# Lower halves of w2 moved from GpSimd to VectorE, the flag sums one half step later, an item's last tile scaled and stored by ScalarE

## The chip, the cores and the metric

One core of a Trainium2 chip runs the whole program. The metric is the device time of one execution in microseconds (us), the median of several runs. Engines are named as in the profile: PE is TensorE, PEld its weight loads, DVE is VectorE, ACT is ScalarE, POOL is GpSimd, SP is the engine that issues most DMAs.

## The reference, cut to what matters

A random-feature attention (4 batches, 8 heads, 576 positions, head size 64, 128 features) gives x of 2304 rows by 512. A mixture of 8 experts follows, one expert for each row:

```python
logits = x @ w_gate
expert_idx = np.argmax(logits, axis=1)
gate_w = probs[np.arange(N), expert_idx]        # softmax of logits
disp[e, counts[e]] = x[i]                       # up to `capacity` rows an expert
h = np.maximum(np.einsum('ecd,edf->ecf', disp, w1), 0.0)
y = np.einsum('ecf,efd->ecd', h, w2)
out[i] = gate_w[i] * y[expert_idx[i], pos[i]]   # zero where not kept
```

## The kernel before, in words

The first half (to about 103 us) is the attention. Its rows x are written to DRAM (x_d). Then come the *items*: a block of 576 rows (one batch) that is run through one expert, j = 0 to 3. Item 0 (block 0, with the expert of its first row) is started before the routing is known; how many of the other blocks have rows for the expert of their first row, and which expert that is, is found on the device by `route()`. The program branches on that count (L802); in this profile items 0, 1 and 2 run and item 3 doesn't. Rows that no item covers would go through lists (L930 and on), a branch that isn't taken here.

An item has two parts. In the first, `mm1` (L607) makes h = relu(x w1) in 16 *half steps*: 8 columns f of 128, and for each two halves of 288 rows. Every product is made as three matmuls, upper times upper, lower times upper and upper times lower (L614 to L616), where the *upper part* of a tile is its rounded copy (ACT, L125) and the *lower part* the rest (a subtraction, L128). A half step is 12 matmuls; then ACT writes the upper part of h (L619, and L621 in second halves) and DVE the lower (L622). In the second part, `mm2_rest` (L754) and `mm2` (L742) multiply by w2, one tile of 128 rows (the rest: 64) after another. `finish` (L769) scales a tile by its gate weights and `put` (L807) stores it. Between these tiles the next item's rows, which `prefetch` (L810) has loaded to xg, are transposed by PE (L347) and split by ACT (L351) and DVE (L353), and its w1 is split.

The lower parts of w2 (four pieces of 128x1024) are placed by the table LO_AT: piece c of w2 is split after column f. For item 0 they run on POOL (L840), for the others on DVE.

Item 0's half steps are interleaved with `route()`: after each, `listing(5)` (L788) takes up to five of its steps, and a step that yields "pe" ends the batch, so that what follows stands behind the next half step. `route()` makes the counts and gate weights on DVE (L369 to L444), spreads the weights to `sc_b` on ACT (L453), makes flags (L456, L458), and PE sums these flags over the rows with one small matmul, called `fs` (L462, preceded by "pe" at L459). From the sums DVE makes the numbers in `resd` (L465 to L510): which expert and which block each further item has. SP loads them (L814, L815) and issues the loads of xg (L338) and of w1 and w2 (L315) for item 1. All engines run their instructions in the order in which the program issues them; there is no scheduler that reorders.

At an item's end `finish` scales tile 3 (i == NSUB - 2) half on ACT (L779) and half on DVE (L781), and SP stores it. The order in which tiles are finished is 4, 0, 1, 2, 3.

```python
                for i, c in LO_AT[j > 0].get(f, ()):
                    split_w_lo(i, c, nc.gpsimd if j == 0 else nc.vector)
```

Of the kernel before, what the change touches and what calls it, by code (L numbers as in the profile page):

```python
# [14 lines left out]
ALU = mybir.AluOpType  # L15
# [4 lines left out]
B, H, S, D, M = 4, 8, 576, 64, 128  # L20
N, DM, E, FF = B * S, H * D, 8, 1024
# [3 lines left out]
SLOTS = 576  # L25
FIRST_CUTS = [0, 128, 384, 768, 1152]
SUB = 128
NSUB = 5
# [11 lines left out]
WARM = 3  # L40

HI_AT = ({2: ((2, 0),), 3: ((2, 1),), 4: ((2, 2),), 5: ((2, 3),)}, {0: ((2, 0),), 1: ((2, 1),), 3: ((2, 2),), 4: ((2, 3),)})
LO_AT = ({2: ((2, 0),), 3: ((2, 1),), 4: ((2, 2),), 5: ((2, 3),)}, {1: ((2, 0),), 2: ((2, 1),), 5: ((2, 2),), 6: ((2, 3),)})


def pause(n):
# [5 lines left out]
def attention_moe(ctx, tc, kT, qT, va, om, wg, w1, w2, cap, ident, tri, desc, lst, tab0, out):  # L52
    nc = tc.nc
# [12 lines left out]
    def bank(i, name):  # L66
        return ps.tile([128, 512], F32, tag=f"b{i}", name=name, bufs=1)
# [36 lines left out]
    resd = const.tile([1, 3, 4], I32, name="resd")  # L104
# [22 lines left out]
    def split_lo(lo, raw, hi, eng=None):  # L127
        (eng or nc.vector).tensor_tensor(lo, raw, hi.bitcast(F32), op=ALU.subtract)  # L128
# [156 lines left out]
    def zero_out(k):  # L285
        if k == 0:
            nc.sync.dma_start(out[SLOTS : SLOTS + REST, :], zero_sb[0:REST, :])
            return
        t = NSUB + 3 * (k - 1)
        z = min(t + 3, NT)  # L290
        nc.sync.dma_start(
            out[t * 128 : z * 128, :].rearrange("(a p) d -> p a d", p=128),
            zero_sb.unsqueeze(1).to_broadcast([128, z - t, DM]),
        )
# [15 lines left out]
    def load_w(i, c, ev):  # L310
        if i == 1:
            src = w1[ds(ev, 1), :, c * 256 : (c + 1) * 256].rearrange("o (k p) f -> p (o k) f", p=128)
        else:
            src = w2[ds(ev, 1), c * 256 : (c + 1) * 256, :].rearrange("o (k p) f -> p (o k) f", p=128)
        nc.sync.dma_start(w_raw[i][c], src)  # L315

    def split_w_hi(i, c, eng=None):
        split_hi(w_hi[i][c], w_raw[i][c], eng)

    def split_w_lo(i, c, eng=nc.vector, k=None):  # L320
        sl = slice(None) if k is None else slice(k, k + 1)
        split_lo(w_lo[i][c][:, sl, :], w_raw[i][c][:, sl, :], w_hi[i][c][:, sl, :], eng)
# [14 lines left out]
    def load_x(row):  # L337
        nc.sync.dma_start(big["xg"], x_d[ds(row, SUB * NSUB), :].rearrange("(i p) d -> p i d", p=SUB))  # L338
# [21 lines left out]
    def route():  # L360
# [21 lines left out]
        src, step = oh, 1  # L382
        while step < T:
# [4 lines left out]
            src, step = dst, 2 * step  # L388
# [68 lines left out]
        yield  # L457
        nc.vector.tensor_scalar(fl[:, 0 : B * NSUB], sc_b.rearrange("p b i -> p (b i)"), 0.0, None, op0=ALU.is_gt)  # L458
        yield "pe"  # L459
        fs = bank(SM, "fs")  # L460
        nf = B * NSUB + T
        nc.tensor.matmul(fs[:, 0:nf], ones_b, fl, start=True, stop=True)  # L462
# [144 lines left out]
    def mm1(f, n, hhi, hlo, hf, nm):  # L607
        xhi, xlo = big["xhi"], big["xlo"]
        whi_, wlo_ = w_hi[1][f // 2], w_lo[1][f // 2]
        fs = slice((f % 2) * 128, (f % 2) * 128 + 128)  # L610
        sl = slice(n * HS, (n + 1) * HS)
        pt = bank((2 * f + n) % 3, f"h{nm}{f}{n}")[:, 0:HS]
        for k in range(4):
            nc.tensor.matmul(pt, whi_[:, k, fs], xhi[:, k, sl], start=(k == 0), stop=False)  # L614
            nc.tensor.matmul(pt, wlo_[:, k, fs], xhi[:, k, sl], start=False, stop=False)  # L615
            nc.tensor.matmul(pt, whi_[:, k, fs], xlo[:, k, sl], start=False, stop=(k == 3))  # L616
        w = HS if n == 0 else HS - REST
        sl = slice(n * HS, n * HS + w)
        nc.scalar.activation(hhi[:, f, sl], pt[:, 0:w], AF.Relu)  # L619
        if n == 1:  # L620
            nc.scalar.activation(hf[:, f, :], pt[:, w:HS], AF.Relu)  # L621
        nc.vector.scalar_tensor_tensor(  # L622
            hlo[:, f, sl], pt[:, 0:w], 0.0, hhi[:, f, sl].bitcast(F32), op0=ALU.max, op1=ALU.subtract
        )

    def h_tiles(nm):
        return [
            hpool.tile([128, 8, w], dt, tag=t, name=f"{t}{nm}")
            for t, w, dt in (("hhi", 4 * SUB, F32R), ("hlo", 4 * SUB, F32R), ("hf", REST, F32))
        ]  # L630
# [7 lines left out]
    for n in range(NK + NT + 3):  # L638
# [6 lines left out]
        elif t < NT:  # L645
            pj = [bank((2 * t + i) % 3, f"pjq{n}{i}") for i in range(2)]
            c = max(i for i in range(len(QB) - 1) if QB[i] <= t)
# [121 lines left out]
    def finish(i, pt, nm, scale, put):  # L769
        n = sub_n[i]  # L770
        y = hpool.tile([SUB, DM], F32, tag="y", name=f"ys{nm}{i}", bufs=3)
        src = pt
        if n < SUB:
            src = y
            nc.scalar.copy(y[0:n, :], pt[n : 2 * n, :])
            nc.vector.tensor_tensor(y[0:n, :], pt[0:n, :], y[0:n, :], op=ALU.add)

        c = DM // 2 if i == NSUB - 2 else DM
        nc.scalar.mul(y[0:n, 0:c], src[0:n, 0:c], scale[0:n])  # L779
        if c < DM:  # L780
            nc.vector.tensor_scalar(y[0:n, c:], src[0:n, c:], scale[0:n], None, op0=ALU.mult)  # L781
        put(i, n, y)


    il = chain(*(g for g, _ in tasks), route())
    stop = [None]

    def listing(n):  # L788
        stop[0] = None
        for _ in range(n):  # L790
            if stop[0] is None:
                stop[0] = next(il, 0)
                if stop[0] == 0:
                    return

    row, nd, nl = None, None, None
    with ExitStack() as ifs:
        for j in range(B):
            nm = f"i{j}"
            last = j == B - 1  # L800
            if j > 0:
                ifs.enter_context(tc.If(nd > j - 1))  # L802
            hhi, hlo, hf = h_tiles(nm) if j > 0 else h0
            out_j = out[0:SLOTS, :] if j == 0 else out[ds(row, SLOTS), :]
            sc = sc_b[:, 0, :] if j == 0 else sc_j[:, j - 1, :]

            def put(i, n, y, out_j=out_j):  # L807
                nc.sync.dma_start(out_j[i * SUB : i * SUB + n, :], y[0:n, :])

            def prefetch():  # L810
                nonlocal row
                if last:
                    return
                ev = nc.sync.value_load(resd[0:1, 0, j : j + 1], min_val=0, max_val=E - 1)  # L814
                row = nc.sync.value_load(resd[0:1, 1, j : j + 1], min_val=0, max_val=N - S)  # L815
                load_x(row)
                for c in range(4):
                    load_w(1, c, ev)
                yield
                for c in range(4):  # L820
                    load_w(2, c, ev)
                yield

            pre = prefetch()
            if j > 0:
                next(pre, 0)
            h = 0
            for f in range(8):
                for half in range(2):
                    if j > 0 or (f, half) not in AHEAD:  # L830
                        mm1(f, half, hhi, hlo, hf, nm)
                        h += 1
                        if j == 0:
                            listing(5)
                for i, c in HI_AT[j > 0].get(f, ()):
                    split_w_hi(i, c)
                if j == 0 and f < 6:
                    zero_out(f)
                for i, c in LO_AT[j > 0].get(f, ()):
                    split_w_lo(i, c, nc.gpsimd if j == 0 else nc.vector)  # L840
            if j == 0:
                for _ in il:
                    pass
                next(pre, 0)
            for n, i in enumerate((NSUB - 1, *range(NSUB - 1))):
                pt = mm2(i, hhi, hlo, nm) if n > 0 else mm2_rest(hf, nm)
                if n == 0:
                    next(pre, 0)
                    finish(i, pt, nm, sc[:, i : i + 1], put)
                if n < 4 and not last:  # L850
                    split_w_hi(1, n)
                if n > 0:
                    finish(i, pt, nm, sc[:, i : i + 1], put)
                if not last:
                    for _ in transpose_x(n, f"i{j + 1}", SM if n % 2 else None):
                        pass
                if n < 4 and not last:
                    split_w_lo(1, n)
            if j == 0:
                nd = nc.values_load(resd[0:1, 2, 0:1], min_val=0, max_val=B - 1)  # L860
                nl = nc.values_load(resd[0:1, 2, 1:2], min_val=0, max_val=N)
# [154 lines left out]
```

## Time and profile before

| | us |
|---|---|
| median of 3 runs (283.48, 284.91, 285.92) | 284.91 |
| the profiled execution, its own time | 284.08 |
| its span, first to last instruction | 282.2 |

A row of a timeline gives the start and the busy time in us, engine, line, operation, output and inputs, the shape, and in brackets the idle time of the engine just before it and what ended that. A row of waits gives the total, the times and the longest. The granted clock of PE is given as a share of its full 2.4 GHz, so 0.50 is 1.2 GHz. Starts and ends of matmuls are modelled and overlap: in a steady stream the distance of two starts is what counts.

### The profile page before, as it was taken

To read this page: it belongs to the slowest core of one execution; us is meant where nothing else is said; L and a number is where in the kernel's file an instruction comes from. 1 tells how busy PE (TensorE), PEld (TensorE's weight loads), DVE (VectorE), ACT (ScalarE), POOL (GpSimd) and SP (SyncE) were. 2 spreads that over 40 slices of the span, in tenths; PEclk is the share of its full clock that TensorE was granted. 3 is DMA by queue.
4 is the path that set the end of the run, shared out by engine and by line. 5 is a ranking of instruction groups with operands and counts; after the bars stand their busy time and mean duration, and the time that the engine had idled before them with its cause. 6 is when DMAs were issued, how large, how long until landed. Compare 5 with 4: busy or idle time off the path is not lost.

```text
span 282.2 us, 7654 instructions
## 1 busy us (share of the span) xinstructions
PE 267.4 (95%) x3106; PEld 234.4 (83%) x3106; DVE 155.5 (55%) x326; ACT 150.0 (53%) x374; POOL 46.2 (16%) x58
## 2 busy tenths in 40 slices
PE   7899999999999999988999999999999999999980
PEld 5688898889899898978868889996888999958860
DVE  1998888678899875774523234443442262514230
ACT  1788778898899874344353415342731345343320
POOL 2100000233379890063300000000000000000000
PEclk9999999999999999997999999999999999999997
DMA  6999760046876844690598015901720293045111
GB/s 187 373 363 302 268 220 5 2 151 179 273 241 225 288 172 130 222 353 4 170 360 312 37 63 183 313 2 58 259 77 37 52 364 107 0 150 202 42 42 51
DMA packets 28450, 48.26 MB, mean 171 GB/s; under 512 B 2098, under 2 KB 14770, under 8 KB 28402
## 3 DMA queue, kind: packets, MB, share of 16 engines
q1 hardware_dynamic: 28258, 47.58, 50.1%
q8 instruction: 28, 0.46, 0.7%
q14 instruction: 20, 0.16, 0.2%
q10 hardware_dynamic: 144, 0.07, 0.1%
HBM read 35.71 MB, written 11.93 MB: 169 GB/s over the span
## 4 chain that ended last, share of the span: by engine, by line
PE 86%; DMA 5%; DVE 2%; issue 2%; ACT 1%; SPq 1%; DVEq 0%; ACTq 0%
PE hi L614 9%; PE hi L615 9%; PE hi L616 9%; PE kacc L212 7%; PE yi L747 7%; PE yi L749 7%; PE yi L748 7%; PE qacc L577 6%; PE pjq L158 6%; PE pjk L158 6%; PE qtr L658 3%; PE xtri L347 3%; DMA kraw<-kT 2%; DMA qraw<-qT 2%; PE yi2r L759 1%
## 5 line engine op out<-in xcount | busy, mean ns | idle before, releaser
L614 PE MATMUL hi<-xhi,w1hi 128*128 128x288 f32 x192 | 58.2, 303 | 0.0
L615 PE MATMUL hi<-xhi,w1lo 128*128 128x288 f32 x192 | 57.3, 299 | 0.0
L616 PE MATMUL hi<-xlo,w1hi 128*128 128x288 f32 x192 | 57.1, 297 | 0.0
L619 ACT ACTIVATE hhii<-hi 128x288 fp32r<-128x288 f32 (+1 forms) x48 | 18.4, 384 | 46.6 <-PE hi L616 46.6
L622 DVE SCALAR_TENSOR_TENSOR hloi<-hi,hhii 128x288 fp32r<-128x288 f32 (+1 forms) x48 | 20.3, 423 | 40.1 <-ACT hfi L621 24.3
L747 PE MATMUL yi<-w2hi,hhii 128*128 128x512 f32 x96 | 38.5, 401 | 0.0
L749 PE MATMUL yi<-w2lo,hhii 128*128 128x512 f32 x96 | 37.5, 391 | 0.0
L748 PE MATMUL yi<-w2hi,hloi 128*128 128x512 f32 x96 | 37.3, 389 | 0.0
L614 PEld LDWEIGHTS hi<-xhi,w1hi 128*128 128x128 f32 x192 | 36.7, 191 | 0.4
L615 PEld LDWEIGHTS hi<-xhi,w1lo 128*128 128x128 f32 x192 | 36.7, 191 | 0.0
L616 PEld LDWEIGHTS hi<-xlo,w1hi 128*128 128x128 f32 x192 | 36.7, 191 | 0.0
L353 DVE TENSOR_TENSOR xlo<-xtri,xhi 128x512 fp32r<-128x512 f32 (+1 forms) x20 | 12.7, 634 | 36.9 <-ACT xhi L351 36.9
L699 POOL TENSOR_TENSOR d<-d,mx 128x512 f32<-128x512 f32 x18 | 18.7, 1039 | 57.6 <-DVE mx L164 43.8
L164 DVE TENSOR_REDUCE mx<-pjk 128x4 f32<-128x512 f32 x36 | 23.1, 683 | 7.2 <-PE pjk L158 6.9
L685 ACT ACTIVATE ex<-pjk,mx 128x128 f32<-128x128 f32 x72 | 20.5, 368 | 8.0 <-DVE mx L164 7.8
L158 PE MATMUL pjk<-om_s,kraw 64*128 64x128 f32 x288 | 22.2, 291 | 2.1 <-DMA kraw<-kT 1.3
L577 PE MATMUL qacc<-kv_sb,qpT 128*64 128x73 f32 x576 | 22.5, 229 | 0.1
L212 PE MATMUL kacc<-v,ex 128*64 128x65 f32 (+1 forms) x576 | 22.3, 230 | 0.0
L158 PEld LDWEIGHTS pjk<-om_s,kraw 64*128 64x128 f32 x288 | 18.3, 192 | 4.7 <-DMA kraw<-kT 2.0
L158 PE MATMUL pjq<-om_s,qraw 64*128 64x128 f32 x288 | 21.0, 284 | 0.7 <-DMA qraw<-qT 0.7
L749 PEld LDWEIGHTS yi<-w2lo,hhii 128*128 128x128 f32 x96 | 18.0, 188 | 3.9
L212 PEld LDWEIGHTS kacc<-v,ex 128*64 128x64 f32 x576 | 19.8, 137 | 1.8 <-issue 1.2
(134 smaller groups left out, 410.8 us busy)
## 6 DMA issues: line engine op xcount, KB each, us to landing
w1raw<-w SPq DMA_DIRECT2D x16, 512.0 KB, 8.3
w2raw<-w SPq DMA_DIRECT2D x16, 512.0 KB, 5.4
qraw<-qT SPq DMA_DIRECT2D x6, 768.0 KB, 6.9
x_d<-xr SPq DMA_DIRECT2D x18, 256.0 KB, 2.8
v<-va SPq DMA_DIRECT2D x7, 650.0 KB, 7.3
kraw<-kT SPq DMA_DIRECT2D x7, 576.0 KB, 7.2
xg<-x_d SPq DMA_DIRECT2D x3, 1280.0 KB, 6.4
out<-zero_sb SPq DMA_DIRECT2D x4, 768.0 KB, 6.2
```

The lines of the kernel that those rows point to most:

```text
L158: nc.tensor.matmul(banks[i][:, k * M : (k + 1) * M], x[rows, :], om_s[rows, :], start=True, stop=True)
L164: nc.vector.tensor_reduce(mx[:, 4 * i : 4 * i + 4], src, op=ALU.max, axis=AX.X, negate=True)
L212: nc.tensor.matmul(acc[f : f + 64, i * 2 * VW + o : i * 2 * VW + o + (z - a) * VW], ex[:, 4 * i + k, f : f + 64], v[:, i, a * VW : z * VW] ...
L577: nc.tensor.matmul(acc[r : r + 64, i * 512 + p * ROW : i * 512 + (p + 1) * ROW], qpT[:, r // 64, (4 * i + p) * 64 : (4 * i + p) * 64 + 64] ...
L614: nc.tensor.matmul(pt, whi_[:, k, fs], xhi[:, k, sl], start=(k == 0), stop=False)
L615: nc.tensor.matmul(pt, wlo_[:, k, fs], xhi[:, k, sl], start=False, stop=False)
L616: nc.tensor.matmul(pt, whi_[:, k, fs], xlo[:, k, sl], start=False, stop=(k == 3))
L622: nc.vector.scalar_tensor_tensor(hlo[:, f, sl], pt[:, 0:w], 0.0, hhi[:, f, sl].bitcast(F32), op0=ALU.max, op1=ALU.subtract)
L685: nc.scalar.activation(ex[:, k, :], pj[0][:, k * M : (k + 1) * M], AF.Exp, bias=mx[:, k : k + 1], scale=1.0)
L747: nc.tensor.matmul(pt, hhi[:, f, sl], w2hi, start=(f == 0), stop=False)
L748: nc.tensor.matmul(pt, hlo[:, f, sl], w2hi, start=False, stop=False)
L749: nc.tensor.matmul(pt, hhi[:, f, sl], w2lo, start=False, stop=(f == 7))
```

## The change

Three edits. The lower parts of w2 for item 0 go from POOL, after columns 2 to 5, to DVE, after columns 6 and 7. `route()` yields "pe" twice ahead of `fs`, so the flag sums and all that follows in `route()` stand one half step later. Tile 3 of an item is scaled whole by ACT and stored by a DMA that ACT issues; for items from 1 on ACT reads the block's row into a register of its own (row_a) at the item's start.

```diff
-LO_AT = ({2: ((2, 0),), 3: ((2, 1),), 4: ((2, 2),), 5: ((2, 3),)}, ...)
+LO_AT = ({6: ((2, 0),), 7: ((2, 1), (2, 2), (2, 3))}, ...)
...
         nc.vector.tensor_scalar(fl[:, 0 : B * NSUB], sc_b.rearrange("p b i -> p (b i)"), 0.0, None, op0=ALU.is_gt)
         yield "pe"
+        yield "pe"
         fs = bank(SM, "fs")
...
-        c = DM // 2 if i == NSUB - 2 else DM
-        nc.scalar.mul(y[0:n, 0:c], src[0:n, 0:c], scale[0:n])
-        if c < DM:
-            nc.vector.tensor_scalar(y[0:n, c:], src[0:n, c:], scale[0:n], None, op0=ALU.mult)
+        nc.scalar.mul(y[0:n, :], src[0:n, :], scale[0:n])
         put(i, n, y)
...
+            if j > 0:
+                row_a = nc.scalar.value_load(resd[0:1, 1, j - 1 : j], min_val=0, max_val=N - S)
-            out_j = out[0:SLOTS, :] if j == 0 else out[ds(row, SLOTS), :]
+            out_j = [out[0:SLOTS, :]] * 2 if j == 0 else [out[ds(r, SLOTS), :] for r in (row, row_a)]
...
             def put(i, n, y, out_j=out_j):
-                nc.sync.dma_start(out_j[i * SUB : i * SUB + n, :], y[0:n, :])
+                k = int(i == NSUB - 2)
+                (nc.sync, nc.scalar)[k].dma_start(out_j[k][i * SUB : i * SUB + n, :], y[0:n, :])
...
                 for i, c in LO_AT[j > 0].get(f, ()):
-                    split_w_lo(i, c, nc.gpsimd if j == 0 else nc.vector)
+                    split_w_lo(i, c)
```

What this moves on three engines is shown by the issue order. A name like hi050 is the result of item 0, column 5, half 0. Line numbers after the change are one higher from the second "pe" on, up to the edit in `finish`.

PE in item 0, at the flag sums, before:

```order
L616 MATMUL hi041_2458<-xlo_993,w1hi2_980 128x288
L462 LDWEIGHTS ones_b_80 [waits DVE_49]
L462 MATMUL fs_2474<-rtfl_2455,ones_b_80 128x38 [waits PE_49]
L614 MATMUL hi050_2491<-xhi_992,w1hi2_980 128x288 [waits PE_49,Activation_49]
L615 MATMUL hi050_2491<-xhi_992,w1lo2_984 128x288
```

and after:

```order
L617 MATMUL hi050_2474<-xlo_993,w1hi2_980 128x288
L463 LDWEIGHTS ones_b_80
L463 MATMUL fs_2489<-rtfl_2453,ones_b_80 128x38 [waits DVE_49]
L615 MATMUL hi051_2503<-xhi_992,w1hi2_980 128x288
L616 MATMUL hi051_2503<-xhi_992,w1lo2_984 128x288
```

`fs` stood between the half steps (4,1) and (5,0) and stands between (5,0) and (5,1): the 12 matmuls of (5,0) come ahead of the wait for DVE.

DVE at the end of item 0's first part, before (hloi is the lower part of h, ysi a tile of the output):

```order
L622 SCALAR_TENSOR_TENSOR hloi0_2147<-hi060_2542,hhii0_2146 128x288 [waits Activation_49]
L515 TENSOR_TENSOR rtw4_2557<-sc_b_97,rtti_2506 128x15 x3
L522 TENSOR_REDUCE sc_j_98<-rtw4_2557 128x15 [waits DVE_49]
L622 SCALAR_TENSOR_TENSOR hloi0_2147<-hi061_2562,hhii0_2146 128x224 [waits PE_49,Activation_49]
L622 SCALAR_TENSOR_TENSOR hloi0_2147<-hi070_2578,hhii0_2146 128x288 [waits Activation_49]
L622 SCALAR_TENSOR_TENSOR hloi0_2147<-hi071_2593,hhii0_2146 128x224 [waits PE_49,Activation_49]
L776 TENSOR_TENSOR ysi04_2645<-yi0r_2632,ysi04_2645 64x512 [waits Activation_49]
```

and after:

```order
L623 SCALAR_TENSOR_TENSOR hloi0_2147<-hi061_2553,hhii0_2146 128x224 [waits PE_49,Activation_49]
L516 TENSOR_TENSOR rtw4_2569<-sc_b_97,rtti_2519 128x15 x3
L523 TENSOR_REDUCE sc_j_98<-rtw4_2569 128x15 [waits DVE_49]
L128 TENSOR_TENSOR w2lo0_2302<-w2raw0_986,w2hi0_2298 128x1024 [waits Pool_49]
L623 SCALAR_TENSOR_TENSOR hloi0_2147<-hi070_2575,hhii0_2146 128x288 [waits Activation_49]
L623 SCALAR_TENSOR_TENSOR hloi0_2147<-hi071_2590,hhii0_2146 128x224 [waits PE_49,Activation_49]
L128 TENSOR_TENSOR w2lo1_2303<-w2raw1_987,w2hi1_2299 128x1024 [waits DMAHW2_49]
L128 TENSOR_TENSOR w2lo2_2304<-w2raw2_988,w2hi2_2300 128x1024 [waits DMAHW5_49]
L128 TENSOR_TENSOR w2lo3_2305<-w2raw3_989,w2hi3_2301 128x1024 [waits DMAHW0_49]
L777 TENSOR_TENSOR ysi04_2645<-yi0r_2632,ysi04_2645 64x512 [waits Activation_49]
```

The end of `route()` stands behind (6,1) instead of (6,0), and four subtractions of 128x1024 are new on DVE, three of them directly ahead of the first tile of the output. POOL has none of them any more.

ACT at the end of item 1, before:

```order
L779 ACTIVATE ysi12_3244<-yi12_3218,sc_j_98 128x512 [waits DMAHW1_49,PE_49,Activation_49]
L351 CAST xhi_992<-xtri23_3247 128x4x128 [waits PE_49]
L779 ACTIVATE ysi13_3280<-yi13_3255,sc_j_98 128x256 [waits DMAHW2_49,PE_49,Activation_49]
L351 CAST xhi_992<-xtri24_3284 128x4x64 [waits PE_49]
L797 COMPARE_AND_BRANCH
L619 ACTIVATE hhii2_3292<-hi200_3318 128x288 [waits PE_49]
```

and after:

```order
L778 ACTIVATE ysi12_3252<-yi12_3226,sc_j_98 128x512 [waits DMAHW1_49,PE_49,Activation_49]
L351 CAST xhi_992<-xtri23_3255 128x4x128 [waits PE_49]
L778 ACTIVATE ysi13_3288<-yi13_3263,sc_j_98 128x512 [waits DMAHW2_49,PE_49,Activation_49]
L809 ISA
L809 DMA out<-ysi13_3288 128x512 [waits DMAHW4_49,DMAHW5_49,DMAHW3_49,Activation_49]
L351 CAST xhi_992<-xtri24_3291 128x4x64 [waits PE_49]
L794 COMPARE_AND_BRANCH
L802 TENSOR_LOAD resd_99
L802 ISA x2
L620 ACTIVATE hhii2_3299<-hi200_3334 128x288 [waits PE_49]
```

The store stands on ACT between the scaling of tile 3 and the last split of the next item's rows, and it waits for ACT's own scaling and for earlier DMAs. SP's queue loses that store, so the next item's loads stand directly behind the store of tile 2 there.

## Rows read from the trace of the kernel before

**Rows 1.** Page, part 1: busy us (share of the span), instructions.

```profile
PE 267.4 (95%) x3106; PEld 234.4 (83%) x3106; DVE 155.5 (55%) x326; ACT 150.0 (53%) x374; POOL 46.2 (16%) x58
```

**Rows 2.** Waits of the whole span: us in total, times, longest.

```profile
PEld xtri L347 <- DMA xg<-x_d: 0.8, 1, 0.8
PE pjq L158 <- DMA qraw<-qT: 0.7, 1, 0.7
```

**Rows 3.** Timeline of PE, half steps (4,1), fs, (5,0) and the start of (5,1).

```profile
123.97 0.29 PE L614 MATMUL hi<-xhi,w1hi 128*128 128x288 f32 x1
...
125.43 0.29 PE L616 MATMUL hi<-xlo,w1hi 128*128 128x288 f32 x1
128.20 0.21 PE L462 MATMUL fs<-rtfl,ones_b 128*128 128x38 bf16 x1 [2.48 <-DVE rtfl L458]
...
131.31 0.36 PE L614 MATMUL hi<-xhi,w1hi 128*128 128x288 f32 x1
```

**Rows 4.** Timeline of DVE ahead of fs.

```profile
123.40 0.23 DVE L433 TENSOR_SCALAR rtk<-pos_e,cap_f 128x18 f32<-128x18 f32 x1
...
124.09 2.40 DVE L439 TENSOR_SCALAR rtm<-rtm 128x18 f32<-128x18 f32 x1
...
127.96 0.18 DVE L458 TENSOR_SCALAR rtfl<-sc_b 128x20 bf16<-128x20 f32 x1 [0.69 <-ACT sc_b L453]
```

**Rows 5.** Timeline of POOL, the second of its four w2lo pieces.

```profile
124.07 2.38 POOL L128 TENSOR_TENSOR w2lo<-w2raw,w2hi 128x1024 fp32r<-128x1024 f32 x1 [1.25 <-ACT w2hi L125]
```

**Rows 6.** Windows: stretch, length, PE, PEld, DVE, ACT, POOL busy, granted clock, DMA share, GB/s.

```profile
88.00:96.00 8.00, 7.30 (x171) 6.89 (x168) 7.08 (x18) 6.95 (x20) 7.35 (x10) 1.00 0.88 282
...
128.20:131.30 3.10, 3.10 (x13) 3.10 (x14) 1.01 (x8) 1.16 (x3) 1.86 (x1) 0.50 0.00 0
```

**Rows 7.** DMA issues of line L338 (ns min/median/max, first and last start), and landing.

```profile
L338 SPq DMA_DIRECT2D xg<-x_d x3: 398/400/415, 136.0 to 223.5; - x3
...
DMA to landing us min/median/max: 6.2/6.4/6.6
```

**Rows 8.** Chain that ended last, where item 0's second part begins: start, us.

```profile
139.49 3.58 PE yi0r L759 x16
143.07 0.59 PE xtri L347 x4
```

**Rows 9.** Groups of DVE by shape: busy us, mean ns.

```profile
L128 DVE TENSOR_TENSOR w2lo<-w2raw,w2hi 128x1024 fp32r<-128x1024 f32 x8 | 9.7, 1217 | 0.0
```

**Rows 10.** Timeline of ACT, DVE and PE at the end of item 0.

```profile
161.04 0.69 ACT L779 ACTIVATE ysi<-yi,sc_b 128x512 f32<-128x512 f32 x1 [3.85 <-issue]
...
166.94 0.47 ACT L779 ACTIVATE ysi<-yi,sc_b 128x256 f32<-128x256 f32 x1 [4.74 <-issue]
...
167.32 0.36 ACT L351 CAST xhi<-xtri 128x256 fp32r<-128x256 f32 x1
...
167.85 0.41 DVE L353 TENSOR_TENSOR xlo<-xtri,xhi 128x256 fp32r<-128x256 f32 x1
...
169.13 0.29 PE L616 MATMUL hi<-xlo,w1hi 128*128 128x288 f32 x1
```

**Rows 11.** ACT's one DMA issue (line L249), in ns.

```profile
L249 ACTq DMA_DIRECT2D om_sb<-om x1: 393/393/393, 0.7 to 0.7; - x1
```

**Rows 12.** The chain's piece on SP beside it: start, us.

```profile
0.75 0.41 SPq L194
```

**Rows 13.** DMA issues of w1raw from 130 to 172 us, in ns.

```profile
L315 SPq DMA_DIRECT2D w1raw<-w x5: 389/444/1127, 136.6 to 171.8; - x5
```

**Rows 14.** Line L930, the last branch: its compare-and-branch and what follows, in ns.

```profile
L930 SPq EVENT_SEMAPHORE  x9: 17/17/17, 279.9 to 280.5; - x9
...
L930 DVEq EVENT_SEMAPHORE  x2: 21/21/21, 279.9 to 280.0; - x2
...
L930 DVEq COMPARE_BRANCH  x1: 69/69/69, 275.5 to 275.5; - x1
L930 SPq COMPARE_BRANCH  x1: 50/50/50, 276.3 to 276.3; - x1
```

More of the change, by code (lines that the diff above doesn't have):

```diff
@@ L42 @@
 HI_AT = ({2: ((2, 0),), 3: ((2, 1),), 4: ((2, 2),), 5: ((2, 3),)}, {0: ((2, 0),), 1: ((2, 1),), 3: ((2, 2),), 4: ((2, 3),)})
-LO_AT = ({2: ((2, 0),), 3: ((2, 1),), 4: ((2, 2),), 5: ((2, 3),)}, {1: ((2, 0),), 2: ((2, 1),), 5: ((2, 2),), 6: ((2, 3),)})
+LO_AT = ({6: ((2, 0),), 7: ((2, 1), (2, 2), (2, 3))}, {1: ((2, 0),), 2: ((2, 1),), 5: ((2, 2),), 6: ((2, 3),)})
 def pause(n):
@@ L794, in listing @@
                     return
-    row, nd, nl = None, None, None
+    row, row_a, nd, nl = None, None, None, None
     with ExitStack() as ifs:
```

## The prediction

> **What bounds the kernel now.** I read the page's engine shares first: PE is busy for 95% of the span [rows 1], so only what PE waits for, what slows it, and what lies behind its last matmul can move the time. The waits view comes second. PE has few waits left: the longest is the one ahead of fs, 2.48 us [rows 3]; then a weight load that is put down to xg, 0.8 us, and one for qraw, 0.7 us [rows 2]. Third, the timeline around fs. The starts of half step (4,1) go from 123.97 to 125.43 in 11 steps, 0.133 us each, so a half step takes 12 of them, 1.59 us, and fs could have started at 125.56. It started at 128.20 [rows 3]: 2.64 us late. fs and the half step behind it took from 128.20 to 131.31, 3.11 us, and the windows view shows why: the granted clock is 0.50 there, the lower level of 1.2 GHz [rows 6]. PE had stood for 2.48 us before. With 1.59 for the half step and 0.1 for fs (38 columns, my estimate) it would have been 1.69, so 1.42 us go to the clock.
>
> Why was fs late? It waits for the flags (L458), written from 127.96 to 128.14. Up the DVE queue one instruction stands out: L439, an addition on 128x18 numbers, took 2.40 us, while L433, of the same kind and shape, took 0.23 [rows 4]. It began at 124.09 and ended at 126.49. POOL's subtraction for w2lo ran from 124.07 to 126.45 [rows 5]. I take it that L439 stood behind POOL's instruction.
>
> **The first edit, w2lo from POOL to DVE, and the second, fs a half step later.** They act on the same place. Without POOL's work L439 should end near 124.09 + 0.23 = 124.32. From its end to the end of L458 it took 128.14 - 126.49 = 1.65 us, so the flags would be there near 126.0. fs alone in its old place would still have waited some 0.4 us (126.0 against 125.56). In its new place PE first runs (5,0) and comes to it at 125.56 + 1.59 = 127.15: a cover of 1.1 us. So the wait of 2.64 us goes, and with it, I think, the slow stretch: -2.64 - 1.42 = -4.06 us. For the wait the bounds are 0 (the cover is used up) and -2.64; for the clock 0 and -1.42.
>
> On the clock a rule speaks for caution. The rows show 13 matmuls at 0.50 in this one execution [rows 6]. The Trainium skill (TensorE: Matmul & The Clock Gate, Part 1: The HAM clock gate) says that the gate isn't tied to the kernel's own start, so that the number of slow matmuls differs from run to run of one kernel. By the row this term is -1.42; by the rule it could be 0 in some executions. That is rival B below.
>
> What is late next? The numbers in resd, and so the loads for item 1, stand one half step later: relative to PE +1.59. The load of xg was issued at 136.0 [rows 7]; now 136.0 + 1.59 - 4.06 = 133.5. It lands 6.2 us after its issue at the earliest [rows 7], so at 139.7 to 139.9. PE used xg first right behind the 16 matmuls of mm2_rest: they began at 139.49 and the transposes at 143.07, with no gap between [rows 8]; 136.0 + 6.2 = 142.2, so xg was there 0.8 us ahead, and the 0.8 us in the waits view cost nothing. After the change PE comes there at 143.07 - 4.06 = 139.0 and waits until about 139.8: +0.9 us (0.4 to 1.3). Of the 4.06 us that much is given back. PE has stood for 0.7 us for qraw [rows 2], in the stretch from 88 to 96 us, with a granted clock of 1.00 [rows 6], so I expect no fall here.
>
> The four subtractions cost DVE 1.22 us each [rows 9]. The first stands behind (6,1), the other three behind (7,1); DVE gets to those about 1 us after PE has finished (7,1), near 136.3, and is done near 139.9. PE needs the first piece at about 140.3, the second 6 matmuls later, and so on: all are there. Behind them in DVE's queue stands the addition for tile 4 (L776), some 0.2 us late, and on PE nothing waits for it before the second tile's products, six microseconds on. I cost this part at 0. The loads of w2 for item 1 now wait for DVE in place of POOL, until 139.9; they are needed 30 us later.
>
> **The third edit, inside the program.** At the end of items 0 and 1 ACT scales 512 columns in 0.69 us instead of 256 in 0.47, from 166.94 to 167.63, then waits for itself and issues the store, and only then makes the last xhi. No row shows ACT issuing a store; its one DMA issue took 0.39 us [rows 11], and SP's for w1raw took up to 1.13 [rows 13]. With 0.39 the cast begins near 168.1, ends at 168.5 (0.36), and xlo is done near 168.95 (0.41). The half step that needs it reads xlo first at 169.13 [rows 10]: 0.2 us to spare. With 1.13 it would be 0.55 late at each of the two ends. I take 0.05 each, +0.1 in all; bounds 0 and 1.1. The store's other waits are on earlier DMAs, among them the store of tile 2, issued some 6 us earlier. ACT's new register load delays the next item's first hhii by about half a microsecond, with three PSUM tiles of slack.
>
> **The third edit, at the program's end.** Before, SP issued the last store and reached the last branch at 276.3; it went on at 279.9, and DVE, there at 275.5, also at 279.9 [rows 14]. These 3.6 and 4.4 us are the branch itself. After the change SP is done with its stores 6 us earlier and has its branch behind it. ACT's cast and DVE's last subtraction come some 0.6 us later (the longer scaling and the issue), so DVE comes to its branch near 276.1 and leaves it between 279.7 (3.6) and 280.5 (4.4); SP has fewer semaphores left to pass when it does (nine of them took from 279.9 to 280.5). I take -0.3 us; bounds -0.9 and +0.3.
>
> **Sum.** -2.64 - 1.42 + 0.9 + 0.1 - 0.3 = -3.36, say -3.4 us. The profiled execution took 284.08 (a span of 282.2 and 1.9 around it), which would become 280.7. The median of the three runs lies 0.8 higher, at 284.91; against it I forecast 281.5.
>
> **The rivals.**
> A: the wait for xg drops the clock again. Against it: the 0.7 us stand for qraw with a clock of 1.00. For it: it follows a stage with half-width weights. Price 1.42 more: 282.9.
> B: in most executions the fall of the clock behind fs doesn't take place, so nothing is won there. Against it: the shown times lie at 283.5 to 285.9 and the profile, with the slow stretch in it, at 284.1. Price: 281.5 + 1.42 = 282.9.
> C, the slower side: SP now reaches the loads of xg and the four of w1raw just when ACT issues its store, and ACT's issue gets behind them. Five issues are 0.4 + 4 x (0.39 to 1.13), 2.0 to 4.9 us, 3.5 in the middle. Then xhi is 3.5 - 0.2 = 3.3 us late, PE stands for as long, and the clock falls as behind fs: 4.7 us at each of two ends, 9.4 in all: 291. From an issue of about 2.3 us on (2 x 1.7 = 3.4 lost) the change would be slower than before. Against it: at the start ACT issued its load in 0.39 us [rows 11] while SP issued in 0.41 us beside it [rows 12].
> D: L439 isn't held by POOL and stays at 2.40 us. Then the flags come at 128.14 and PE waits 1.0 us at the new place, about as much as xg would cost anyway: 2.64 - 1.0 + 1.42 won, less 0.3 to 1 for xg, now later: 282.4. L439's end 0.04 us behind POOL's speaks against it. The Trainium skill (SBUF — State Buffer, SBUF: two separate sides) has the two engines share one pair of ports, held for a whole instruction; the trace agrees, and by that rule D has a chance of 0.05, no more.
> E: xg is in time after all (a faster landing, or resd sooner): 280.6.
>
> **How the numbers follow.** Forecast 0.62, A 0.12, B 0.08, C 0.05, D 0.05, E 0.08. About 1% is what a measurement of this kernel can tell from no change; that is below 282.06. The forecast's terms spread it by some 0.8 us: about three quarters of its chance is below, and all of E: 0.47 + 0.08, and 0.03 from B and D: 0.58 faster. Slower by over 1% is C and a little of the rest: 0.06. Between lie 0.36. The range takes the terms' good ends together (-2.64 - 1.42 + 0.4 - 0.9 = -4.6, 280.3, less 0.6 for the runs' own spread) and on the other side A or B with a late store (282.9 + 1.1 = 284.0): 279.7 to 284.1.
>
> **What would show it right or wrong.** Right: L439 at about 0.2 us; no idle time of PE ahead of fs and a clock of 1.00 there; a wait of 0.4 to 1.3 us for xg ahead of item 0's second part; no new wait of PE at the start of items 1 and 2; SP at its last branch several us earlier, DVE last. Wrong: fs still waiting, a window at 0.50 near the transposes (A), ACT's DMA issue at over 1 us with hi waiting for xhi (C), or a median above 284.1.

## The result, and the profile after

The first comparison gave 280.33 us (median of six runs) beside 283.70 for the kernel before (six), a ratio of 0.985, 95% interval 0.980 to 0.990: faster by 1.5%. Runs over 1.5% above the fastest of their kernel count as disturbed and are left out of every ratio and of the medians below; of the changed kernel's first six that is one, at 433.7 us. 0.985 of 283.70 is 279.4, just under the low end of my range. Over all other runs of this study the medians are 283.92 before (72 runs) and 280.35 after (24): 3.57 us, where I forecast 3.4. The profiled execution took 280.86 us, a span of 279.1, against 284.08 and 282.2.

Page, part 1 [rows 1]: PE's busy time is 1.1 us shorter, and POOL has lost its four subtractions (46.2 to 36.7 us).

```profile
PE 266.3 (95%) x3106; PEld 233.5 (84%) x3106; DVE 154.9 (56%) x327; ACT 151.2 (54%) x374; POOL 36.7 (13%) x54
```

PE's waits of the whole span [rows 2], (us in total, times, longest): fs is gone from the list, xg is new for PE itself.

```profile
PE ktr L232 <- DVE kv_sb L247: 1.3, 1, 1.3
...
PE xtri L347 <- DMA xg<-x_d: 0.9, 1, 0.9
...
PE pjq L158 <- DMA qraw<-qT: 0.3, 1, 0.3
```

Timeline of DVE ahead of fs [rows 4]. L439 begins as before and takes 0.18 us in place of 2.40; the flags (L458) are written from 125.95.

```profile
124.10 0.18 DVE L439 TENSOR_SCALAR rtm<-rtm 128x18 f32<-128x18 f32 x1
...
125.95 0.18 DVE L458 TENSOR_SCALAR rtfl<-sc_b 128x20 bf16<-128x20 f32 x1 [0.69 <-ACT sc_b L453]
```

Timeline of PE [rows 3, 8]: the counts' matmul `pos`, from which I count below because all kernels do the same up to it; fs, 0.14 us behind the start of the matmul ahead of it, with no idle time; and the beginning of item 0's second part, where the wait for xg has appeared.

```profile
120.36 0.24 PE L396 MATMUL pos<-oh,tri_b 128*128 128x144 bf16 x1
...
127.03 0.29 PE L617 MATMUL hi<-xlo,w1hi 128*128 128x288 f32 x1
127.17 0.19 PE L463 MATMUL fs<-rtfl,ones_b 128*128 128x38 bf16 x1
127.20 0.38 PE L615 MATMUL hi<-xhi,w1hi 128*128 128x288 f32 x1
...
135.33 3.65 PE L760 MATMUL yi0r<-w2raw,hfi 128*64 128x512 f32 x16
139.85 0.66 PE L347 MATMUL xtri<-id_sb,xg 128*128 128x128 f32 x4 [0.86 <-DMA xg<-x_d]
```

Windows around fs and around that wait [rows 6] (length, busy times, granted clock, DMA share, GB/s): the clock is 1.00 in all of them, the upper level.

```profile
125.40:128.60 3.20, 3.20 (x26) 3.13 (x25) 1.33 (x9) 2.31 (x7) 0.00 (x0) 1.00 0.37 133
128.60:131.80 3.20, 3.20 (x27) 3.20 (x26) 2.04 (x11) 1.82 (x4) 0.00 (x0) 1.00 0.00 0
136.00:142.00 6.00, 5.14 (x26) 2.56 (x23) 4.36 (x5) 1.82 (x3) 0.00 (x0) 1.00 1.06 372
```

The issues of xg [rows 7]: the first is at 133.5 (before 136.0), and it lands after 6.3 us.

```profile
L338 SPq DMA_DIRECT2D xg<-x_d x3: 407/407/414, 133.5 to 217.6; - x3
...
DMA to landing us min/median/max: 6.3/7.3/8.1
```

ACT and DVE at the end of item 0 [rows 10]. ACT's store issue takes 0.36 us; xlo is ready at 165.75, and PE's first matmul that reads it there starts at 165.99, without idle time.

```profile
163.80 0.69 ACT L778 ACTIVATE ysi<-yi,sc_b 128x512 f32<-128x512 f32 x1 [4.74 <-issue]
164.52 0.36 ACTq L809 DMA_DIRECT2D out<-ysi  x1
164.92 0.37 ACT L351 CAST xhi<-xtri 128x256 fp32r<-128x256 f32 x1 [0.44 <-ACT ysi L778]
...
165.33 0.42 DVE L353 TENSOR_TENSOR xlo<-xtri,xhi 128x256 fp32r<-128x256 f32 x1 [4.41 <-ACT xhi L351]
...
165.99 0.29 PE L617 MATMUL hi<-xlo,w1hi 128*128 128x288 f32 x1
```

The last branch [rows 14]. SP reaches it at 267.0 in place of 276.3; DVE at 273.1, and it goes on 4.5 us later, at 277.6. DVE is now the last.

```profile
L931 DVEq EVENT_SEMAPHORE  x2: 21/21/21, 277.6 to 277.7; - x2
...
L931 SPq COMPARE_BRANCH  x1: 50/50/50, 267.0 to 267.0; - x1
...
L931 DVEq COMPARE_BRANCH  x1: 69/69/69, 273.1 to 273.1; - x1
```

### The profile page after: what moved, and what is told of

Same layout as the page of the kernel before. It is cut to its first block, busy times and chain, and to the rows that moved or that the text cites. A ratio compares the mean times of both kernels' runs of the same rounds, so it can differ in the third digit from the quotient of the medians.

```text
span 279.1 us, 7654 instructions
## 1 busy us (share of the span) xinstructions
PE 266.3 (95%) x3106; PEld 233.5 (84%) x3106; DVE 154.9 (56%) x327; ACT 151.2 (54%) x374; POOL 36.7 (13%) x54
## 5 line engine op out<-in xcount | busy, mean ns | idle before, releaser
L615 PE MATMUL hi<-xhi,w1hi 128*128 128x288 f32 x192 | 57.5, 300 | 0.0
L616 PE MATMUL hi<-xhi,w1lo 128*128 128x288 f32 x192 | 56.7, 296 | 0.0
L617 PE MATMUL hi<-xlo,w1hi 128*128 128x288 f32 x192 | 56.4, 294 | 0.0
L615 PEld LDWEIGHTS hi<-xhi,w1hi 128*128 128x128 f32 x192 | 36.0, 188 | 0.4
L617 PEld LDWEIGHTS hi<-xlo,w1hi 128*128 128x128 f32 x192 | 36.1, 188 | 0.0
L616 PEld LDWEIGHTS hi<-xhi,w1lo 128*128 128x128 f32 x192 | 36.1, 188 | 0.0
L578 PEld LDWEIGHTS qacc<-kv_sb,qpT 128*64 128x64 f32 x576 | 20.0, 136 | 1.7 <-issue 0.5
```

The source lines that it names most:

```text
L578: nc.tensor.matmul(acc[r : r + 64, i * 512 + p * ROW : i * 512 + (p + 1) * ROW], qpT[:, r // 64, (4 * i + p) * 64 : (4 * i + p) * 64 + 64] ...
```

## The experiments

My theory: POOL's subtraction held L439, that made PE stand ahead of fs, and the stand cost the clock; of that gain 0.86 us went to xg. Rivals: only the cover of the later place matters; the clock's fall has another cause; the rest of the gain is edit 3's, or the spread of runs.

Each row of the table is one profiled execution, in us: from the start of pos to the start of fs, to the first transposes of item 1 (xtri) and to the end of PE's last matmul; and the *tail* from there to the start of the program's last instruction, which takes 0.05 us. The median is over all runs that count, with their number.

| kernel | fs | xtri | last matmul | tail | median (runs) |
|---|---|---|---|---|---|
| before | 7.85 | 22.66 | 153.76 | 8.00 | 283.92 (72) |
| after | 6.81 | 19.49 | 150.61 | 8.05 | 280.35 (24) |
| e1_lo: edit 1 alone | 5.83 | 19.24 | 150.34 | 7.91 | 280.24 (6) |
| e2_pe: edit 2 alone | 7.86 | 24.16 | 155.27 | 8.31 | 286.93 (12) |
| e5_poollate: edits 2, 3 | 7.86 | 24.19 | 156.89 | 7.49 | 285.89 (10) |
| e3_store: edit 3 alone | 7.85 | 22.65 | 153.75 | 7.50 | 283.26 (12) |
| e6_fill: before, PE filled | 7.87 | 23.54 | 156.24 | 7.83 | 286.43 (6) |
| e7_half: before, POOL in halves | 7.30 | 21.79 | 152.89 | 8.28 | 283.03 (12) |
| e12_nostore: edits 1, 2 | 6.81 | 19.49 | 150.59 | 8.48 | 280.74 (12) |
| v1_list9: after, nine steps | 6.81 | 18.56 | 149.66 | 7.87 | 279.38 (17) |
| v2: v1 without edit 3 | 6.81 | 18.56 | 149.66 | 8.26 | 279.96 (12) |

**Edit 1 alone** (e1_lo):

```diff
-LO_AT = ({2: ((2, 0),), 3: ((2, 1),), 4: ((2, 2),), 5: ((2, 3),)}, ...)
+LO_AT = ({6: ((2, 0),), 7: ((2, 1), (2, 2), (2, 3))}, ...)
...
-                    split_w_lo(i, c, nc.gpsimd if j == 0 else nc.vector)
+                    split_w_lo(i, c)
```

> Edit 1 alone (w2's lower parts of item 0 on DVE after columns 6 and 7; the flag sums in their old place; tile 3 as before). Theory (the wait ahead of fs came from POOL's instruction and took the clock with it): L439 at about 0.2 us, flags written near 126.0, fs starts near 126.2 in place of 128.20, so PE still stands about 0.5 us there; that short stand doesn't lower the clock. The numbers for item 1 come a half step sooner than in the changed kernel, so xg costs 0 to 0.2 us in place of 0.86. PE's last matmul at about 270.8 us, the span 278.5 to 279.2, about 3.2 us under the kernel before. Rival (the half step of cover is what matters): fs waits 1.5 us or more, the clock falls, and the gain is under 1.5 us. Rival (a stand of 0.5 us is enough to lower the clock): the wait goes, but 1.4 us stay lost: gain about 2 us.

Measured: ratio 0.986 (0.981 to 0.990). PE's timeline: fs waits 0.45 us, xg no more.

```profile
125.90 0.19 PE L462 MATMUL fs<-rtfl,ones_b 128*128 128x38 bf16 x1 [0.45 <-DVE rtfl L458]
...
139.30 0.66 PE L347 MATMUL xtri<-id_sb,xg 128*128 128x128 f32 x4
```

Up to the last matmul it is 3.42 us ahead of before, 0.27 ahead of the whole change. Edit 1 alone makes the gain; behind it edit 2 trades 0.45 us at fs for 0.86 at xg.

**Edit 2 alone** (e2_pe):

```diff
         yield "pe"
+        yield "pe"
         fs = bank(SM, "fs")
```

> Edit 2 alone (the flag sums a half step later; w2's lower parts still on POOL after columns 2 to 5; tile 3 as before). Theory: L439 stays at 2.4 us behind POOL's piece, the flags come at 128.14, fs stands at 127.15 in PE's order and starts near 128.25: a wait of 1.0 us. The clock stays up after so short a stand. xg is issued near 134.5 and lands near 141, PE comes to it near 140.1 and waits 0.6 to 1.7 us. PE's last matmul near 272.1, the span near 280.2: about 2 us under the kernel before, 1.1 over the changed kernel. Rival (a stand of 1 us lowers the clock): 1.4 us less gain, 0.6 us under before.

Measured: ratio 1.008 (1.004 to 1.011), slower than before, where I expected it 2 us faster. The wait at fs was as expected (0.90), but DVE's timeline shows POOL's next pieces, back to back, on the instructions that make item 1's numbers:

```profile
130.98 4.75 POOL L128 TENSOR_TENSOR w2lo<-w2raw,w2hi 128x1024 fp32r<-128x1024 f32 x2 [2.99 <-ACT w2hi L125]
...
131.62 0.17 DVE L466 TENSOR_REDUCE rtnb<-fs 128x4 f32<-128x20 f32 x1
...
131.83 1.59 DVE L473 TENSOR_SCALAR rton<-rtnb 128x3 f32<-128x3 f32 x1
...
133.46 2.30 DVE L477 TENSOR_TENSOR rtn<-rton 128x3 f32<-128x3 f32 x1
```

Behind them a half step waits 1.54 us for hloi, xg is issued at 139.3, 17.5 us behind pos (before: 15.7), and PE waits for it:

```profile
136.32 0.41 PE L615 MATMUL hi<-xhi,w1hi 128*128 128x288 f32 x1 [1.54 <-DVE hloi L623]
...
146.03 0.66 PE L347 MATMUL xtri<-id_sb,xg 128*128 128x128 f32 x4 [2.67 <-DMA xg<-x_d]
```

Up to the last matmul this execution is 1.51 us longer than before, half of the 3.0 us between the medians. In nine of the twelve runs, at 286.8 to 288.2, the mean granted clock is 0.982 to 0.988, in the other three, at 284.4 to 285.1, 0.992 to 0.994. The stretch at 0.50 of the profiled one lies at its start (11.06 to 14.48); that most of the others have it behind xg, as e5_poollate and e6_fill below, would fit, but no trace of this kernel shows it.

So a later place is no cover by itself: it moves the routing's short instructions under another of POOL's pieces.

**POOL's work at the late places** (e5_poollate): the changed kernel with `nc.gpsimd if j == 0 else nc.vector` back in the call.

> The changed kernel, but w2's lower parts of item 0 run on POOL again, at the changed kernel's places (after columns 6 and 7). Theory (what matters is when POOL's big instruction runs, not which engine makes the lower parts): L439 at 0.2 us and no wait ahead of fs, as in the changed kernel. POOL's pieces of 2.4 us each now begin near 131.5 and 136 and run to about 143.5, and DVE's instructions beside them are stretched by up to 2.3 us each: resd and xg may come up to 2 us later, and the last piece stands ready about 3.5 us later than on DVE, which PE needs only behind 18 matmuls of the first tile. I expect 0.5 to 3 us slower than the changed kernel. Rival (POOL's instruction doesn't hold DVE; DVE's load by other work did): L439 long again or no stretched DVE instruction near 131 to 143.

Measured: ratio 1.006 (1.002 to 1.009). The edit did not do what I meant. POOL has nothing else to do there and starts each piece when its input is there, wherever it stands in the program: the first two began at 120.12 and 123.75, 0.10 and 3.73 us behind pos, as before [rows 5]. The kernel is edits 2 and 3, and its waits are those of e2_pe (2.74 us for xg). Behind that one the clock fell to 0.50 (144.73 to 148.14), and from xtri to the last matmul it took 132.7 us, where e2_pe and every kernel without such a stretch there took 131.1: a fall there costs its whole 1.6 us. Whether POOL's work would do harm later was not tried.

**POOL's pieces in halves** (e7_half), everything else as before:

```diff
-                    split_w_lo(i, c, nc.gpsimd if j == 0 else nc.vector)
+                    for k in (0, 1) if j == 0 else (None,):
+                        split_w_lo(i, c, nc.gpsimd if j == 0 else nc.vector, k)
```

> The kernel before with each of POOL's four subtractions of 128x1024 made as two of 128x512. Theory (a DVE instruction on SBUF alone that starts beside POOL's waits for the end of that one instruction): L439 takes 1.2 us in place of 2.40, and the flags come up to 1.2 us sooner, unless POOL's second half goes first and holds the next instruction of that kind (L441, L444 or L456) another 1.2 us. fs then starts 6.7 to 7.85 us behind pos, and PE's last matmul comes 0 to 1.2 us sooner. Rival (DVE is held for POOL's whole piece of work, or for another reason): L439 stays at 2.40.

Measured: ratio 0.995 (0.992 to 0.998). POOL's second piece, and DVE beside it:

```profile
123.77 2.52 POOL L128 TENSOR_TENSOR w2lo<-w2raw,w2hi 128x512 fp32r<-128x512 f32 x2 [1.09 <-ACT w2hi L125]
...
123.79 1.31 DVE L439 TENSOR_SCALAR rtm<-rtm 128x18 f32<-128x18 f32 x1
125.13 0.27 DVE L441 RECIPROCAL pay<-rtm 128x18 f32<-128x18 f32 x1
125.31 0.39 DVE L622 SCALAR_TENSOR_TENSOR hloi<-hi,hhii 128x288 fp32r<-128x288 f32 x1
125.63 0.70 DVE L444 TENSOR_TENSOR rtc<-rto,pay 128x18 f32<-128x18 f32 x1
```

The halves take 1.29 and 1.27 us; L439 ends 0.03 us behind the first one, and L444 ends at 126.33, 0.04 behind the second. The delay is what is left of POOL's running instruction: the theory, with both of its branches. This settles what held L439.

**The clock** (e6_fill): ahead of fs in the kernel before, where PE stood, matmuls whose result nobody reads.

```diff
         yield "pe"
+        pf = bank(3, "fill")[:, 0:HS]
+        for k in range(18):
+            nc.tensor.matmul(pf, w_hi[1][2][:, 0, 0:128], big["xhi"][:, 0, 0:HS], start=(k == 0), stop=(k == 17))
         fs = bank(SM, "fs")
```

> The kernel before with 18 matmuls of 288 columns, whose result nobody reads, ahead of fs: they fill PE's 2.4 us of waiting there (18 x 0.133). Nothing else is changed, so fs still starts near 128.2. Theory (the slow stretch behind fs comes from PE's stand): the granted clock stays 1.00, the half step behind fs takes 1.6 us in place of 3.1, and the kernel is about 1.4 us faster than before, ratio 0.995. Rival B (the fall of the clock isn't in most executions, or isn't tied to the stand): ratio 1.000, or a stretch at 0.50 in spite of the matmuls.

Measured: ratio 1.008 (1.005 to 1.012). The clock stayed at 1.00 behind fs, and yet the kernel is slower. (That the filled stand kept it up is not shown: in e3_store, below, it stayed at 1.00 behind the stand itself.) DVE's part of the half step behind fs comes 1.4 us sooner after pos, and so DVE reaches L510 (the numbers of the further items' experts) just when POOL's fourth piece begins; xg is 2.2 us late, and behind that stand the clock falls after all, and costs 1.6 us as in e5_poollate:

```profile
132.88 2.40 POOL L128 TENSOR_TENSOR w2lo<-w2raw,w2hi 128x1024 fp32r<-128x1024 f32 x1 [1.38 <-ACT w2hi L125]
```
```profile
132.90 2.40 DVE L510 CAST resd<-rtrf 1x3 int32<-1x3 f32 x1
...
143.52 0.92 PE L347 MATMUL xtri<-id_sb,xg 128*128 128x128 f32 x4 [2.17 <-DMA xg<-x_d]
```
```profile
125.00:130.00 5.00, 4.89 (x38) 4.66 (x37) 3.07 (x14) 2.30 (x8) 2.00 (x2) 1.00 0.24 88
143.70:147.10 3.40, 3.40 (x11) 2.81 (x11) 0.46 (x1) 2.12 (x3) 0.00 (x0) 0.51 1.10 355
```

**Edit 3 alone** (e3_store): `finish`, `put` and `row_a` as in the change, LO_AT, the call and `route()` as before.

> Edit 3 alone (tile 3 scaled whole and stored by ACT; w2's lower parts and the flag sums as before). Theory: ACT's store issue takes 0.37 us as in the changed kernel, no wait of PE at the item ends, tail behind the last matmul within 0.1 us of 8.0: no change, ratio 1.000 within 0.002. Rival (tail term): 0.3 us faster. Rival (the store's issue or its landing gets in the way of the next item's loads): slower by 0.5 us or more at the item ends.

Measured: ratio 0.997 (0.994 to 1.001), which the runs can't tell from 1. Its trace shows what the clock's fall behind fs was worth with POOL's pieces in place. PE stood as long ahead of fs as before, but the clock did not fall behind it, and the kernel reached the end of the last matmul 153.75 us behind pos, where before, with the fall, it was 153.76:

```profile
126.85 0.19 PE L462 MATMUL fs<-rtfl,ones_b 128*128 128x38 bf16 x1 [2.47 <-DVE rtfl L458]
...
141.66 0.66 PE L347 MATMUL xtri<-id_sb,xg 128*128 128x128 f32 x4 [1.33 <-DMA xg<-x_d]
```
```profile
126.60:129.80 3.20, 2.95 (x22) 2.95 (x23) 1.73 (x11) 1.82 (x4) 1.70 (x1) 1.00 0.01 2
```
```profile
132.01 2.32 DVE L508 TENSOR_SCALAR resd<-rtrf 1x3 int32<-1x3 f32 x1
```

POOL's fourth piece (131.90, 2.41 us) held L508 by 2.2 us, xg was late, and PE waited 1.33 us for it. In the kernel before, the slow stretch kept DVE back until POOL's third piece was over, and the casts to resd got in just ahead of the fourth (L507 to L509; L510, a single number, began 0.02 us behind it and wasn't held):

```profile
134.43 0.15 DVE L507 CAST resd<-rtrf 1x3 int32<-1x3 f32 x1
```
```profile
134.65 2.40 POOL L128 TENSOR_TENSOR w2lo<-w2raw,w2hi 128x1024 fp32r<-128x1024 f32 x1 [2.84 <-ACT w2hi L125]
```

So there the fall cost PE 1.42 us and spared it a wait of 1.33 us for xg; that the two executions end within 0.01 us of each other is chance. More runs point the same way: of the 66 runs of the kernel before with a mean clock on record, 19 have 0.990 to 0.992, near e3_store's profiled run (0.992), and 28 have 0.987 or 0.988, near the profiled run with the fall (0.987). Their medians are 283.6 and 283.9 us, 0.3 apart and not 1.4; which of these runs had the fall there isn't shown.

**Without edit 3** (e12_nostore, pair1_without): edits 1 and 2, `finish` and `put` as before. The mates are the changed kernel again (after_again, after_third, pair1_with).

> Edits 1 and 2 without edit 3. Theory (the store by ACT bought nothing at the end and cost nothing between items): the same as the changed kernel within 0.3 us, in the span and in the ratio. Rival (my prediction's tail term): 0.3 us slower than the changed kernel behind the last matmul, that is, a tail of 8.3 us in place of 8.05.

> The changed kernel once more, beside more runs of the kernel before. If the step of 4.3 us between the medians is the kernels' and my sum of 3.4 was short, the ratio stays near 0.985. If it was the spread of single runs (each kernel's own runs lie 2 to 3 us apart), it moves towards 0.988, which is 3.2 to 3.4 us by the two profiles.

> The changed kernel for the third time, to settle the size of the change and as the mate of the runs beside it. By the traces (3.15 us between pos and the last matmul, tail equal) the ratio is 0.989; a ratio of 0.985 would say that something outside the traces adds 1 us.

> The changed kernel, mate of the next one. Theory (edit 3 is worth about 0.45 us behind the last matmul): the tail is 7.4 to 8.05 us, and the median lies 0.3 to 0.9 us under the mate without edit 3. Rival (edit 3 is worth nothing; earlier medians differ by the spread of runs): medians within 0.3 us of each other.

> Edits 1 and 2 without edit 3. Theory: SP reaches its branch 2.2 us behind PE's last matmul, the tail is 7.9 to 8.5 us, the median 0.3 to 0.9 us over the changed kernel's. Rival: no difference beyond 0.3 us.

Measured: the changed kernel's ratio was 0.989 (0.986 to 0.992), 0.984 (0.980 to 0.987) and 0.990 (0.986 to 0.994); without edit 3 it was 0.987 (0.982 to 0.992) and 0.988 (0.985 to 0.991). Run side by side, pair1's medians agree to 0.04 us (280.65 and 280.69): the rival, by its times.

**The wait for xg taken away** (v1_list9, v1_again, pair2_with; v2_list9_nostore and pair2_without are the same without edit 3):

```diff
-                            listing(5)
+                            listing(5 if f < 5 else 9)
```

> The changed kernel, with up to nine steps of the routing after each half step from column 5 on in place of five, so that the numbers for item 1 are made one half step sooner. Theory (0.86 us of PE's wait for xg are what the late flag sums gave back): xg is issued near 131.9 in place of 133.5, lands near 138.7, PE doesn't wait for it, and the kernel is 0.8 us faster than the changed one, PE's last matmul near 270.1. Rival: the longer batch delays hloi on DVE, and PE waits for a PSUM bank instead: no gain or up to 1 us slower.

> The changed kernel with nine steps of the routing after each half step from column 5 on, once more and beside the changed kernel on the same chip. In the traces it gains 0.95 us from the counts' matmuls (pos) to PE's last matmul, which is 0.3% of the time. If that holds, its median lies 0.9 us under the changed kernel's of this call and the ratio to before near 0.985 to 0.986; if its first look was the spread of runs, the two agree within 0.3 us.

> The changed kernel with nine steps of the routing from column 5 on. Against the changed kernel: 0.5 to 1 us faster (the wait for xg gone, 0.95 us by the traces). Against its mate without edit 3: 0.3 to 0.9 us faster by the theory, within 0.3 us by the rival.

> Edits 1 and 2 and nine steps from column 5 on, without edit 3. Theory (edit 3's only worth is at the program's end, 0.3 us): pos to the last matmul as with edit 3 (149.7 us), the tail behind the last matmul 8.0 to 8.5 us in place of 7.5 to 8.05, the median 0.3 us above the other kernel with nine steps, which these rounds can hardly tell. Rival (edit 3 is worth nothing): tails alike.

> The same with nine steps, without edit 3. Theory: tail 7.9 to 8.5 us, median 0.3 to 0.9 us over its mate. Rival: within 0.3 us.

Measured: with edit 3 0.986 (0.984 to 0.988), 0.981 (0.978 to 0.985) and 0.984 (0.980 to 0.987); without it 0.986 (0.982 to 0.990) and 0.985 (0.982 to 0.988). PE's timeline of v1_again: no wait for xg, which was issued at 131.1, 11.8 us behind pos (after: 13.1).

```profile
134.27 3.65 PE L760 MATMUL yi0r<-w2raw,hfi 128*64 128x512 f32 x16
137.85 0.66 PE L347 MATMUL xtri<-id_sb,xg 128*128 128x128 f32 x4
```

0.95 us less up to the last matmul in each of its three traces, and 0.97 between the medians of 17 and 24 runs. It beats both kernels: 4.5 us (1.6%) under before.

On edit 3 the times don't agree with each other. Side by side, pair2's medians are 279.74 and 279.75, which again is the rival; v2_list9_nostore was 1.44 us above v1_again (280.24 and 278.80). Over the whole study the median without edit 3 is 0.39 us (after) and 0.58 us (v1) higher. Nine traces with edit 3 have tails of 7.39 to 8.05 us, mean 7.71; nine without have 7.82 to 8.48, mean 8.17. The spread comes from the branch, which takes DVE 3.8 to 4.5 us with edit 3 and SP 3.4 to 4.1 without, from one execution to the next. With edit 3 it ends 0.3 us later on average (6.30 against 5.97 us behind the last matmul), but from there on 1.40 us are left with edit 3 and 2.20 without, in every trace. By the tails edit 3 is worth 0.45 us (pair1's and pair2's tails differ by 0.46 each); the times neither confirm nor exclude that.

## Why the prediction was right, and where it failed

- **L439 and POOL.** Right: 0.18 us; e7_half shows the cause. The Trainium skill (SBUF — State Buffer, Who interferes with whom) says that DVE instructions with two inputs in SBUF, and copies, casts and tensor_scalar in their faster modes, contend with POOL, and that on trn2 a tensor_reduce never does. The traces agree in the main: L439, L444, L473, L477, L508 and L510 above (each by the lines of its own kernel) were held, and L424, a reduction of 128x144 numbers in SBUF, took 0.30 us beside POOL's first piece (before) as without it (after). Casts of a single number were not held: one that began 0.02 us behind POOL's fourth piece (before, L510) took 0.13 us.
- **fs and the place.** Right in the sum: fs began at 127.17, forecast 127.15, and PE came to xtri without the wait at 139.0. The half step of cover was not what brought it (e1_lo).
- **xg, +0.9.** It was 0.86, issued at 133.5 as forecast. The sum up to the last matmul, with 0.1 for the store, is -2.64 - 1.42 + 0.9 + 0.1 = -3.06; measured -3.15.
- **The clock, -1.42.** Right in this execution, wrong as a price by itself: I took it for lost time that stands alone. Where the fall doesn't come, POOL's later pieces make PE wait for xg instead (e3_store), and edit 1 takes both away. Rival B's case ("so nothing is won there", 282.9) occurs, as e3_store shows, but its price of 1.42 us was wrong: nearly nothing is lost by it. How often the fall comes in the kernel before stays open.
- **Rival A** (a fall behind the wait for xg). None came behind the 0.86 us, in four traces of the changed kernel and two without edit 3. Behind the waits there of kernels with POOL's pieces it came twice (2.74 and 2.17 us) and three times not (2.67, 1.33 and 1.02); it cost 1.6 us, where I had put 1.42.
- **Rival D** (282.4 if L439 stays at 2.40). L439 didn't stay, so its price wasn't tried. e2_pe has D's wait at fs (0.90 us, forecast 1.0), but POOL's third and fourth pieces, which edit 1 takes away, still ran there and held DVE (1.59 and 2.30 us); its 286.9 is theirs.
- **Inside the program, +0.1.** No wait at the item ends; ACT's issue took 0.36 us, not the 2.3 that rival C needs. (C's own sum is off: by the reckoning for 1.13, an issue of 3.5 us makes xhi 2.9 us late, not 3.3, which gives 290 in place of 291.) DVE's four subtractions cost nothing, as forecast.
- **The tail, -0.3.** The two profiles don't show it (8.00 and 8.05); over eighteen traces it is -0.45.
- **The failed step** is the base: "The median of the three runs lies 0.8 higher, at 284.91; against it I forecast 281.5", with 0.6 us at the low end of the range for the runs' own spread. Three runs don't hold that median: with 72 it is 283.92, 1.0 us lower and below the profiled 284.08, and the standard deviation of one run is 0.95 us. Of the 2.1 us from 281.5 down to 279.4, 1.2 are the base (284.91 against 283.70 in the first comparison). The other 0.9 are the change, 4.3 us by that ratio where I forecast 3.4; the three later comparisons, 0.989, 0.984 and 0.990, suggest that this first one was low in part by chance. The sum itself held: with -3.4 on 283.92 the forecast would have been 280.5, against a median of 280.35. Of its terms the tail was the furthest off, -0.3 against -0.45. Traces and tails together, -3.15 - 0.45 = -3.6, are close to the 3.57 us between the medians, which the spread of the runs leaves uncertain by some 0.3 us (my estimate, from standard deviations of 0.95 us in 72 runs and 1.08 in 24).

## What to carry to other kernels

When a tiny instruction on DVE is slow, look at what POOL runs beside it: the price is the rest of POOL's instruction, and moving the victim can put it under the next one, so take away the long instruction, or cut it. A stretch of slow clock or a wait is worth its length only as far as the next chain leaves room: ahead of the load of xg the clock's fall cost almost nothing here, behind it, where PE waited for nothing more, its whole 1.6 us. Before a gain of 1% is set against a median, count how many runs stand behind that median.

## What I had not expected of the hardware

The clock's fall is not tied to a stand's length alone: stands of 2.47 us (e3_store) and 2.67 (e2_pe) were followed by 1.00, those of 2.48 (before), 2.17 (e6_fill) and 2.74 (e5_poollate) by 0.50 or 0.51, the lower level. The Trainium skill (TensorE: Matmul & The Clock Gate, Part 1: The HAM clock gate) says that the gate isn't tied to the kernel's own start. The traces agree: the same stretch of the changed kernel, shown below, had 0.50 in one execution and 1.00 in another.

Most of the spread between the traces lies in the start. From item 0's first product on, eighteen traces agree to 0.1 us wherever their code is the same (pos comes 16.36 to 16.38 us behind it); but that product starts at 102.6 to 105.5. Windows of pair1_with, where it started at 105.07, and below of the profiled changed kernel, at 104.00:

```profile
9.70:13.00 3.30, 3.30 (x44) 3.08 (x44) 2.18 (x4) 1.97 (x7) 0.41 (x2) 0.50 1.04 406
```
```profile
9.70:13.00 3.30, 3.30 (x79) 3.11 (x80) 3.24 (x6) 2.94 (x9) 0.85 (x5) 1.00 1.03 392
```

Seven of the eighteen traces have such a start, two of the changed kernel and five of other versions: in five the clock fell again for 3.4 us between 9.4 and 14.5 us, in two it first rose only at 13.2 or 13.4. Their first product is at 104.45 to 105.50 us, that of the other eleven at 102.64 to 104.11. The stretch comes ahead of everything that the edits touch and is no part of the change.
